# First rows in two transfers, reordered lists and more fillers in an attention and SwiGLU kernel

## The chip, the cores and the metric

The program runs on one core of a Trainium2 chip. The metric is the device time of one launch in microseconds (us). The kernel before took 363.26 us, the median of three runs (363.25 to 364.06 us).

A core has a matrix engine (TensorE, PE in the profile, with its weight loads as PEld), VectorE (DVE), ScalarE (ACT), GpSimd (POOL) and SyncE (SP, which only issues transfers here). Each engine has its own list of instructions and works through it in order; semaphores hold it back where it needs another engine's result or a transfer. TensorE writes into PSUM, from which VectorE and ScalarE copy.

## The reference

Eight batches of eight heads, 576 tokens each, 64 wide, with 16 beacon keys and values ahead of the 576 causal ones; then a SwiGLU block over the 4608 tokens with 512 model and 1536 inner columns. All is float32 in memory.

```python
k_all = np.concatenate([beacon_k, k], axis=2)
v_all = np.concatenate([beacon_v, v], axis=2)
scores = (1 / sqrt(64)) * q @ k_all.T          # 576 x 592 per batch and head
scores = where(causal, -1e9, scores)           # beacons are seen by every row
a = exp(scores - max); a /= a.sum(-1) + 1e-9
x = (a @ v_all) -> [4608, 512]                 # tokens by (head, width)
out = (silu(x @ w_gate) * (x @ w_val)) @ w_out
```

## The kernel before, in words

**Attention.** The work on a batch is cut into four pairs of heads. For each pair the queries and keys come as rows (tile `qk`), TensorE turns them (`turn`, plan letter T, into `t_ps`), and copies bring them into `qT` and `kT` (`turned_copy`: K and Q on VectorE, k and q on ScalarE). Scores are made in units A to D, four to a pair (letters S and s; s adds the causal mask by further matmuls with `ramp` and `against`). ScalarE takes the exponential of a unit (E) into `p`; where a unit wasn't masked by matmuls, a mask multiplies it on VectorE (D) or GpSimd (M). The product with the values (P and p, tile `pv_ps`; Z for the first 240 rows of batch 0, `pvf_ps`) is normalized on VectorE (R, N) into `x`, and turned into `xT` (X, J, V).

**The SwiGLU block.** One gate and value product (G, then H, both halves into `gv_ps`) makes 128 inner columns for up to 512 tokens. ScalarE takes tanh (a), VectorE multiplies twice (1, 2) into `hT`. The projection (F) collects the 12 blocks of inner columns into two banks of `o_ps`, which `evacuate` copies out (O on VectorE, o on ScalarE) and stores. The last pair of token blocks is projected in two parts of 320 and 192 columns, each in its own bank, so that the first part can be copied while the second is computed.

**What sets the order.** There is no scheduler: `plan` is a string of letters, and each letter emits its piece in that order on whatever engines it uses. `order_of_loads` names the loads that the letters L and l issue one after the other on GpSimd's queue (K0.4: keys of batch 0, heads 4 to 7; v0.2: a block of 128 value rows of batch 0; g2, u2: the third part of the gate and val weights). Eight semaphores serve these loads in turn, so the ninth load waits on GpSimd until the first has landed. The letter h asks for one filler, a matmul of the identity that nobody reads; `keep_warm` emits those asked for ahead of the next score unit or value product.

**PSUM.** Four slots of two banks each go round. `take` gives a tile the slot that has been free for longest, `give` returns it. Dependencies are followed by tile; `apart` declares that two instructions of different engines on one tile don't depend on each other, since they touch different banks.

**The opening.** The first 256 rows of heads 0 and 1 come through SyncE's and ScalarE's queues into `first` (L672), those of heads 2 to 7 by GpSimd (L681). The beacons of batch 0 are cast by VectorE (b), turned (W) and copied (e on ScalarE, A on VectorE). From batch 1 on, two heads are first paired side by side (`pair_up`, g on VectorE, f on GpSimd, into `side`), so that one transpose serves both.

Of the kernel before, what the change touches and what calls it, by code (L numbers as in the profile page):

```python
# [84 lines left out]
def kernel(  # L85
# [733 lines left out]
    pSyEGXRHELDSyLDGaELGH1H2aaXD1Lf2Py1pGGLH2GRaXHlylH12aaGGH112a2HG1G2Haa1HaTq2lgGl1H2k1GaS21l2HSEa
    lsElGS12ETHgKQGEaS12lEHlTDa1GSqH2glDkESfaGslE1H2ElSEMDlTGMSQaKEHSMM12aGEs1HEa2T1qPpMllkDPfllSpRE  # L820
    2sRfsPDpSEEFEFFSFRDFFlSElSPEMpTFFlFERkFSfFFlqDSSFFFlEDFDEFSFTEFDFFFSQVlEkEFFDDFFOSEOllFFTtFqKFDl
    MSFESFFFFElSSMDlFElPplPlpERsFDFRFFFEFStlFFEGSGHtFDHDEaGMF1FFaH12POlOpaPp2RlG1GlRHtal2G1HHGVa21ll
    l2ltGHal1G2lGHHa1aatlt21tGH1H2lattF2aGFH112FF2FFGSaEFlHt1GFFaHa2Gltl1t2GtlH12latH12Fa12FFGGtDHSl
    tlaE1FHFFaG2lSFHtl12allF12GFElMFllFHaSG1FEFHaGFFolMHl2l1G2aSOF1H2FaE1FtFG2sHFEaFslF1FDFlSE2FDFED
    FSESlPpFFFRlDFFFlStFESSDFFEFFsEDFOPEpMPEOpSFFlFRMStRFEFEFSsFEMEFFDFFPplFSFFFFFlFRDSSEFEtFtSFDFFF
    FFEEFlVFFsoOElFFSFtFFDFtSMPEDEtSFElpSDRFFMFFtlMPtESSFEEpRFttFFGFDDSEGHFGa12HHlla1aG21FHl2aGlFHl1
    a2GSHD1ool2aDtPlEGM1ltp2HRlla1GtlSlGH2alEGHG1l2FaM1HHF2a1GFa2HS1FF2FSFFaEFSFEF12lFSPEFpDMFEFSlSR
    FFlEFFtSFttEFFDFSFVFFESEtFFFMsMDEFFFDFEsOFSFFolPttDEFDFSpFFEMFsESFRFFFEFFtFPMEGGOtHoSEtaplHRPtla
    11Gpt2HD2tGMRaGSt1HH2tGEa1al2G1HSa2GEH1a2GttHGa12SHH1a2MEG1GaM2DSHHES12FaEFFFFF1FDla2FFPSF1FE2Fp
    RFFSFFSEFSFESFFFFVEFSFFFFDDFEFFEFFDSoFPFFMlFpFEStlFERFFFFFSSDoEPMFFEFFFDDOMGpoRSElPHGa1S2pHEaR1G  # L830
    2sHlGGEDaHaD12GG1Ha2H12aG1Ha2HaGG12S1EHlHGa2a1D2MSH1FEl2GSMFa1H2EMPaFDF1FSF2EDFFFpSFEFFsRFFFSFFF
    SEFPEEFFSFpERFFSFFFMDVFMSFFDEEPFFDSoFFFFpFFFFEFDOFSPRFDFSpEGFFFEGRGDDFHaO1oHH2aa12P1GpRHGGH2VaGH
    a1a12HG2Ga1H122HGa1Ga2G1HHH2aa1a21G21GH2aG12HaHGFFFF1a2FFGF1H2aHaGF1H2FaF1GF2F1GHHFFFaa2FF12G1GH
    aFFFFH12F2FFFFFFaG1FHFFoFaFoFF212GGFHaFF1FHFF2FFaFGFFFFOHoG12GHHFaa12GFaFFF1FFF21FHF2GGFFaHFaFF1
    FFF12FHa2FG1GFHF2HFaF1FoaFFoFFFFFG2FF1FFHFaF1FGFF2HGFFFaFF12FH2FFaFFFFF1FFFFF2oFFFFFFFFFFFFOFFFF
    FFFOFoFFFFFFFFFFFOoFFFFFFOo
# [43 lines left out]
```

## Time and profile before

| | |
|---|---|
| median of three runs | 363.26 us (363.25 to 364.06) |
| profiled execution | 364.0 us, of it the span 362.0 us |
| TensorE busy | 353.9 us, 98% of the span |
| VectorE, ScalarE, GpSimd busy | 223.6, 189.0, 123.8 us |
| gate and val matmuls, 1824 | 406.2 us of modelled time, two running at once |
| projection matmuls, 912 | 116.0 us |
| mean granted clock | 0.995 of full speed |

Busy time of TensorE is the time in which at least one matmul ran; their ends are modelled, and two on different halves of the array overlap. The waits are read from the timeline (the number in brackets behind a row is the idle time ahead of it and what ended it) and from the table by stage, where the length of a stretch less its busy time is the idle time.

### The profile page before, as it was taken

How to read it: one execution, taken by the hardware profiler on the slowest of the kernel's cores; microseconds unless marked ns; L12 is line 12 of the kernel's file. 1: busy time of each engine (PE TensorE's matmuls, PEld its weight loads, DVE VectorE, ACT ScalarE, POOL GpSimd, SP SyncE). 2: the span in 40 equal slices, each digit the busy share in tenths (PEclk: the TensorE clock that was granted, in tenths of full speed). 3: DMA queues.
4: the chain of work that ended last, by engine and by line, in shares of the span. 5: the costliest groups of instructions: out<-in, count | busy, mean ns of one | idle time of the engine just before them, and what ended most of it. 6: DMA issues, size and time to landing. Idle time of an engine off the chain costs nothing.

```text
span 362.0 us, 11854 instructions
## 1 busy us (share of the span) xinstructions
PE 353.9 (98%) x5150; PEld 200.7 (55%) x5150; DVE 223.6 (62%) x437; ACT 189.0 (52%) x286; POOL 123.8 (34%) x185
## 2 busy tenths in 40 slices
PE   7899999999999999999999999999999999999996
PEld 4677566654444566544565556545655554455554
DVE  5577987667766753497518763777467764464341
ACT  4966989822425677543864466546633332331311
POOL 8935489936337544375423013112000000000000
PEclk9899999999999999999999999999999999999999
DMA  8999999999999999999999829602422000110113
GB/s 120 166 204 203 186 194 139 173 176 155 140 153 113 133 137 119 161 115 170 139 120 170 111 28 138 95 0 20 107 78 67 2 2 0 61 58 3 61 60 116
DMA packets 146132, 39.74 MB, mean 110 GB/s; under 512 B 131488, under 2 KB 141728, under 8 KB 146080
## 3 DMA queue, kind: packets, MB, share of 16 engines
q0 software_dynamic: 97424, 19.00, 73.4%
q1 hardware_dynamic: 48368, 19.76, 26.3%
q8 instruction: 40, 0.66, 0.8%
q10 hardware_dynamic: 288, 0.23, 0.2%
q14 instruction: 12, 0.10, 0.1%
HBM read 38.27 MB, written 9.44 MB: 132 GB/s over the span
## 4 chain that ended last, share of the span: by engine, by line
PE 84%; DMA 8%; POOL 4%; issue 3%; ACT 1%; POOLq 0%
PE gv_ps L173 46%; PE o_ps L173 26%; PE s_ps L173 5%; DMA wv<-in_moe_w_val_dram 4%; PE pv_ps L173 4%; PE pv_ps L505 3%; DMA wg<-in_moe_w_gate_dram 2%; DMA qk<-in_q_dram 2%; POOL qk L215 1%; POOL vb L225 1%; ACT p L414 0%; POOL wv L254 0%; POOL p L427 0%; POOL wo L258 0%; PE t_ps L171 0%
## 5 line engine op out<-in xcount | busy, mean ns | idle before, releaser
L173 PE MATMUL gv_ps<-xT,wv 64*128 64x512 bf16 (+2 forms) x912 | 203.2, 365 | 0.6 <-DMA wv<-in_moe_w_val_dram 0.6
L173 PE MATMUL gv_ps<-xT,wg 64*128 64x512 bf16 (+2 forms) x912 | 203.0, 365 | 0.1
L591 ACT ACTIVATE th<-gv_ps 128x512 f32<-128x512 f32 (+2 forms) x114 | 65.4, 575 | 118.0 <-PE gv_ps L173 117.6
L414 ACT ACTIVATE p<-s_ps 128x832 bf16<-128x832 f32 (+2 forms) x127 | 104.6, 869 | 34.4 <-PE s_ps L173 28.7
L173 PE MATMUL o_ps<-wo,hT 64*128 64x512 bf16 (+2 forms) x912 | 116.0, 365 | 0.4 <-ACT p L414 0.4
L596 DVE SCALAR_TENSOR_TENSOR u<-th,gv_ps 128x512 f32<-128x512 f32 (+2 forms) x114 | 74.7, 656 | 66.4 <-ACT th L591 65.7
L173 PEld LDWEIGHTS <-wg 64*128 64x128 bf16 x912 | 82.4, 94 | 45.7 <-PE gv_ps L173 2.4
L173 PEld LDWEIGHTS <-wv 64*128 64x128 bf16 x912 | 81.7, 94 | 40.7 <-DMA wv<-in_moe_w_val_dram 0.7
L603 DVE SCALAR_TENSOR_TENSOR hT<-gv_ps,u 128x512 bf16<-128x512 f32 (+2 forms) x114 | 74.7, 661 | 3.0
L173 PEld LDWEIGHTS <-hT 64*128 64x128 bf16 x912 | 43.4, 94 | 32.8 <-DVE hT L603 0.7
L225 POOL DMA_DIRECT2D vb<-in_v_dram x40 | 33.9, 851 | 63.0 <-PE s_ps L173 25.3
L173 PE MATMUL s_ps<-qT,kT 64*128 64x336 bf16 (+3 forms) x512 | 43.5, 254 | 1.4 <-ACT kT L262 0.8
L173 PEld LDWEIGHTS <-kT 64*128 64x128 bf16 x512 | 23.8, 94 | 22.6 <-issue 1.4
L423 DVE TENSOR_TENSOR p<-p,ramp 128x256 bf16<-128x256 bf16 (+2 forms) x84 | 23.9, 315 | 10.0 <-ACT p L414 9.8
L225 POOL DMA_DIRECT2D qk<-in_q_dram x25 | 21.2, 851 | 25.5 <-DMA qT<-qk 5.8
L534 DVE TENSOR_TENSOR x<-pv_ps,rec 128x640 bf16<-128x640 f32 (+1 forms) x32 | 25.3, 791 | 1.2
L533 DVE RECIPROCAL rec<-pv_ps 128x10 f32<-128x10 f32 (+1 forms) x32 | 6.8, 213 | 28.8 <-PE pv_ps L173 22.8
L225 POOL DMA_DIRECT2D qk<-in_k_dram x25 | 21.2, 851 | 5.7 <-PE gv_ps L173 4.4
L427 POOL TENSOR_SCALAR_AFFINE_SELECT p<-p 128x256 bf16<-128x256 bf16 (+2 forms) x46 | 17.5, 402 | 13.6 <-ACT p L414 13.3
L263 DVE COPY o_sb<-o_ps 128x512 f32<-128x512 f32 (+2 forms) x18 | 11.6, 657 | 16.5 <-PE o_ps L173 16.5
L173 PEld LDWEIGHTS <-p 64*128 64x128 bf16 x960 | 18.7, 94 | 4.5 <-PE pv_ps L173 0.2
L173 PE MATMUL pv_ps<-vb,p 64*128 64x65 bf16 x960 | 19.9, 189 | 0.0
(63 smaller groups left out, 142.8 us busy)
## 6 DMA issues: line engine op xcount, KB each, us to landing
out_dram<-o_sb SPq DMA_DIRECT2D x34, 256.0 KB, 3.6
vb<-in_v_dram POOLq DMA_DIRECT2D x24, 128.0 KB, 5.8
qk<-in_q_dram POOLq DMA_DIRECT2D x21, 128.0 KB, 5.2
qk<-in_k_dram POOLq DMA_DIRECT2D x16, 128.0 KB, 5.8
wo<-in_moe_w_out_dram POOLq DMA_DIRECT2D x2, 768.0 KB, 9.8
wg<-in_moe_w_gate_dram POOLq DMA_DIRECT2D x3, 384.0 KB, 14.9
wv<-in_moe_w_val_dram POOLq DMA_DIRECT2D x3, 384.0 KB, 13.7
qk<-in_k_dram POOLq DMA_DIRECT2D x2, 576.0 KB, 11.9
```

What stands on the lines that cost most here:

```text
L173: ins = nc.tensor.matmul(o, lhsT=l, rhs=r, start=start, stop=stop)
L225: return nc.gpsimd.dma_start(dst[p0 : p0 + n, c, :, 0:D], src[b, :, r : r + n, :].rearrange("h j d -> j h d"))
L263: return eng.tensor_copy(o, i)
L414: nc.scalar.activation(p_of(b, m, u == "A")[:, :, c0 : c0 + w], ps[:, :, 0:w], ACT.Exp, scale=0.125)
L423: nc.vector.tensor_tensor(out=ap, in0=ap, in1=upper[:, None, d : d + w].to_broadcast([P, 2, w]), op=ALU.mult)
L427: nc.gpsimd.affine_select(out=ap, in_=ap, compare_op=ALU.is_ge, fill=0.0, base=d, pattern=[[0, 2], [1, w]], channel_multiplier=-1,)
L505: ins = nc.tensor.matmul(o_ps[:, side, 68 * c : 68 * c + D + 1], lhsT=pt[n % NPT][:, side, col : col + P], rhs=vb[b % 2][:, t, 2 * m + sid ...
L533: nc.vector.reciprocal(rec[:, :, c0:NKT], o[:, :, :, D : D + 1])
L534: nc.vector.tensor_tensor(out=xs[b][:, c0:NKT, P * m : P * m + P].rearrange("p c (h d) -> p h c d", d=D), in0=o[:, :, :, 0:D], in1=rec[:, ...
L591: nc.scalar.activation(th[:, 0:w], gvs[n][:, 0, 0:w], ACT.Tanh, scale=0.5)
L596: nc.vector.scalar_tensor_tensor(out=u[:, 0:w], in0=ths[n][:, 0:w], scalar=1.0, in1=gvs[n][:, 0, 0:w], op0=ALU.add, op1=ALU.mult)
L603: nc.vector.scalar_tensor_tensor(out=hTs[j][:, f, c0:c1], in0=gvs.pop(n)[:, 1, 0 : c1 - c0], scalar=0.5, in1=ths.pop(n)[:, 0 : c1 - c0], o ...
```

## The change

The first rows of heads 2 to 7 come in two transfers (keys, queries) for four. The plan is ordered anew from its start to about a quarter; behind its first 448 letters (458 now), about 77 us into the span, it is letter for letter the old one. The order of the first 56 loads changes too. In that part the plan has twenty fillers for ten, three key copies more on VectorE and one query copy fewer (three key copies fewer on ScalarE, one query copy more), two copies into `xT` on VectorE that were ScalarE's, five masks on GpSimd that were VectorE's, one paired copy more on GpSimd, and the beacon copy on VectorE. All other letters stand in the same number. The calls of `apart` in `project` and `evacuate` are gone, and `halves` returns nothing.

```diff
@@ halves
         newest[0] = ins.ins.name
-        return ins
@@ project
-                ins = halves(
+                halves(
                     key, at, row, ps[:, at, cols],
 ...
-                if at:
-                    apart(ins, copied.get((key, 0), []))
@@ evacuate
-        ins = copy(eng, o_sb[:, cols], ps[:, at, cols])
-        apart(ins, copied.get((key, 1 - at), []))
-        copied[key, at] = [ins]
+        copy(eng, o_sb[:, cols], ps[:, at, cols])
@@ opening
-    for h0, h1 in ((2, 4), (4, H)):
+    for h0, h1 in ((2, H),):
         runs(0, k, h0, h1, 0, FRONT)
         runs(0, q, h0, h1, 0, FRONT)
@@ order_of_loads
-    K0.0 Q0.0 v0.2 Q0.4 K0.4 v0.1 v0.0 v0.3 v0.4 v0.5 g1 u0 g0 u1 g2 u2 K1 Q1 b1 u3 g3 g4 u4 Q2 v1.5 K2 v1.3
+    v0.0 Q0.0 K0.0 Q0.4 v0.1 K0.4 v0.2 v0.4 v0.3 v0.5 u1 u0 g1 g0 g2 u2 Q1 K1 b1 g3 u3 u4 v1.5 g4 v1.2 v1.0 K2
 ...
@@ plan
-    0LhbTqLLhhWKehTQsLTLEKLsqLkELhhSLTcQsKELKEsLssQEshsEhDELshEEELLhLTQZkNZsNSPpJEEILsJPLLERIpSXLDRP
+    0bWTAqkhhhhsTLLLELcqKThhsqKhhhSTELELqKsDsEKLEhshsQEEsZThsNhhhsEQhhZLLLEKLEsLPpNESREJhhsIELSJPDLp
 ...
```

**TensorE, from the ninth score unit of batch 0 to the first value product.** `s_ps` are scores, `t_ps` the turn of the last key and query rows, `pvf_ps` the value product of the first rows; DMASW0 to DMASW7 are the semaphores of GpSimd's loads. Before:

```order
L187 MATMUL s_ps<-ident 128x256 [waits Activation_49]
L173 LDWEIGHTS kT_107
L173 MATMUL s_ps<-qT_105,kT_107 128x336
...
L171 LDWEIGHTS qk_101 [waits DMASW0_49]
L171 MATMUL t_ps<-ident,qk_101 64x64 [waits Activation_49]
...
L446 LDWEIGHTS p_109 [waits DMASW2_49]
L446 MATMUL pvf_ps<-vb_103,p_109 128x65 [waits DMASW1_49]
...
L446 MATMUL pvf_ps<-vb_103,p_109 128x65 [waits DMASW6_49]
```

And now:

```order
L173 MATMUL s_ps<-against,ramp 128x16
L445 LDWEIGHTS p_109 [waits DMASW6_49]
L445 MATMUL pvf_ps<-vb_103,p_109 128x65 [waits DMASW2_49]
...
L445 MATMUL pvf_ps<-vb_103,p_109 128x65 [waits DMASW0_49]
...
L171 LDWEIGHTS qk_101 [waits DMASW7_49]
L171 MATMUL t_ps<-ident,qk_101 64x64 [waits Activation_49]
...
L186 MATMUL s_ps<-ident 128x256 [waits Activation_49]
L173 LDWEIGHTS kT_107
L173 MATMUL s_ps<-qT_105,kT_107 128x336
```

The value product stands ahead of the turn and of the ninth and tenth score units, no longer behind them. Its last wait, DMASW0, is for the second value block (v0.2).

**GpSimd, the first loads.** Before, in the order in which they are issued behind the first rows of heads 4 to 7:

```order
L215 DMA qk_101<-in_k_dram 64x4x320
L215 DMA qk_101<-in_q_dram 64x4x320
L225 DMA vb_103<-in_v_dram 128x8x64
...
L225 DMA vb_103<-in_v_dram 112x8x64 [waits DMASW1_49]
L225 DMA vb_103<-in_beacon_v_dram 16x8x64 [waits DMASW2_49]
```

And now, from the first transfer on:

```order
L214 DMA qk_101<-in_k_dram 64x6x256
L214 DMA qk_101<-in_q_dram 64x6x256
...
L224 DMA vb_103<-in_beacon_v_dram 16x8x64
L214 DMA qk_101<-in_q_dram 64x4x320
...
L224 DMA vb_103<-in_v_dram 112x8x64
L214 DMA qk_101<-in_k_dram 64x4x320
L224 DMA vb_103<-in_v_dram 128x8x64 [waits DMASW0_49]
```

The 128 value rows (v0.2) move from the third place of the list to the seventh, where the values of the beacons stood; the same six loads are then ahead of the seventh.

**TensorE, the last matmuls.** The last of 320 columns and the first of 192. Before:

```order
L173 MATMUL o_ps<-wo,hT 128x320
L173 LDWEIGHTS hT [waits PE_49]
L173 MATMUL o_ps<-wo,hT 128x192
L173 LDWEIGHTS hT
L173 MATMUL o_ps<-wo,hT 128x192
```

And now:

```order
L173 MATMUL o_ps<-wo,hT 128x320
L173 LDWEIGHTS hT [waits PE_49]
L173 MATMUL o_ps<-wo,hT 128x192 [waits DVE_49]
L173 LDWEIGHTS hT [waits PE_49]
L173 MATMUL o_ps<-wo,hT 128x192 [waits Activation_49]
```

The order is the same; the first matmul into the second part of either tile now waits for VectorE and for ScalarE, which are the copies of the 320 columns.

## Rows read from the trace of the kernel before

**Rows 1.** The page: busy tenths of TensorE in 40 slices of the span.

```profile
PE   7899999999999999999999999999999999999996
```

**Rows 2.** By stage: window, length, busy us (count) by engine, PEclk, DMA, GB/s.

```profile
8.00:10.00 2.00, 1.16 (x48) 0.62 (x46) 0.14 (x1) 2.00 (x4) 2.00 (x4) 1.00 1.54 141
11.50:15.00 3.50, 3.50 (x82) 2.27 (x78) 0.80 (x4) 3.50 (x5) 2.90 (x5) 0.51 2.20 154
25.00:27.00 2.00, 1.44 (x31) 1.18 (x29) 1.69 (x5) 0.19 (x1) 0.00 (x0) 1.00 1.22 209
50.00:60.00 10.00, 9.23 (x202) 6.62 (x203) 7.91 (x16) 8.30 (x14) 9.99 (x17) 1.00 1.71 170
60.00:150.00 90.00, 89.94 (x1250) 49.19 (x1247) 56.26 (x109) 50.31 (x72) 49.16 (x69) 1.00 1.71 148
```

**Rows 3.** The waits of TensorE: total, times, longest us.

```profile
PE pv_ps L505 <- POOL p L427: 0.4, 1, 0.4
```

**Rows 4.** Timeline of GpSimd: start, us, engine, line, operation, idle before.

```profile
1.33 0.71 POOL L215 DMA_DIRECT2D qk<-in_k_dram  x1 [0.81 <-POOLq L864]
...
3.24 0.64 POOL L215 DMA_DIRECT2D qk<-in_q_dram  x1
...
8.53 0.57 POOL L225 DMA_DIRECT2D vb<-in_beacon_v_dram  x1
...
15.89 0.76 POOL L254 DMA_DIRECT2D wv<-in_moe_w_val_dram  x1
...
31.63 1.14 POOL L263 COPY side<-qk 128x1152 bf16<-128x1152 bf16 x1 [7.78 <-DMA qk<-in_q_dram]
```

**Rows 5.** Transfers issued at 3.24, 8.53 and 15.89 us: KB, us to landing.

```profile
qk<-in_q_dram POOLq DMA_DIRECT2D x1, 128.0 KB, 3.9
...
vb<-in_beacon_v_dram POOLq DMA_DIRECT2D x1, 16.0 KB, 5.9
...
wv<-in_moe_w_val_dram POOLq DMA_DIRECT2D x1, 384.0 KB, 10.2
```

**Rows 6.** Timeline of ScalarE, fifth to tenth exponential and the copy behind them.

```profile
11.47 4.81 ACT L414 ACTIVATE p<-s_ps 128x832 bf16<-128x832 f32 x6
16.11 0.77 ACT L262 ACTIVATE kT<-t_ps 128x640 bf16<-128x640 bf16 x1
```

**Rows 7.** Timeline of TensorE: fillers, scores, turn, value product, fourth gate product.

```profile
5.96 0.61 PE L187 MATMUL s_ps<-ident 128*128 128x256 bf16 x4
...
12.84 0.57 PE L173 MATMUL s_ps<-qT,kT 64*128 64x336 bf16 x4
...
14.34 0.75 PE L171 MATMUL t_ps<-ident,qk 64*64 64x64 bf16 x40
...
15.25 0.71 PE L446 MATMUL pvf_ps<-vb,p 128*128 128x65 bf16 x18
...
16.93 0.21 PE L173 MATMUL s_ps<-qT,kT 64*128 64x80 bf16 x2 [0.28 <-ACT kT L262]
...
26.18 0.27 PE L173 MATMUL gv_ps<-xT,wv 64*128 64x240 bf16 x1 [0.56 <-DMA wv<-in_moe_w_val_dram]
```

**Rows 8.** Timeline of VectorE, a copy of the turn and a normalization.

```profile
15.14 0.82 DVE L263 COPY qT<-t_ps 128x640 bf16<-128x640 bf16 x1 [2.84 <-PE t_ps L171]
...
16.11 0.76 DVE L462 TENSOR_TENSOR x<-pvf_ps,rec 128x256 bf16<-128x256 f32 x2
```

**Rows 9.** Timeline of VectorE and ScalarE, one pair of output copies.

```profile
319.53 0.69 DVE L263 COPY o_sb<-o_ps 128x512 f32<-128x512 f32 x1 [2.27 <-PE o_ps L173]
319.53 0.60 ACT L262 ACTIVATE o_sb<-o_ps 128x512 f32<-128x512 f32 x1 [2.21 <-PE o_ps L173]
```

**Rows 10.** Timeline of the end: matmuls of 192 columns, copies of 320.

```profile
357.35 0.49 PE L173 MATMUL o_ps<-wo,hT 64*128 64x192 bf16 x7
...
357.56 0.49 DVE L263 COPY o_sb<-o_ps 128x320 f32<-128x320 f32 x1 [1.92 <-PE o_ps L173]
357.60 0.44 ACT L262 ACTIVATE o_sb<-o_ps 128x320 f32<-128x320 f32 x1 [2.05 <-PE o_ps L173]
```

More of the change, by code (lines that the diff above doesn't have):

```diff
@@ L734 @@
     order_of_loads = """
-    K0.0 Q0.0 v0.2 Q0.4 K0.4 v0.1 v0.0 v0.3 v0.4 v0.5 g1 u0 g0 u1 g2 u2 K1 Q1 b1 u3 g3 g4 u4 Q2 v1.5 K2 v1.3
-    v1.2 v1.0 v1.1 v1.4 b2 o0 o1 v2.2 k3.0 v2.1 q3.2 v2.5 k3.5 v2.4 v2.3 v2.0 q3.4 q3.0 q4.2 k4.0 v3.3 k3.1 q4.0
-    k3.4 k3.2 q3.1 v3.0 k4.2 q3.3 k4.3 v3.5 q4.4 k3.3 v3.4 v3.2 k4.5 k4.1 q4.3 q4.1 v4.1 v4.5 v4.3 v4.0 k4.4
+    v0.0 Q0.0 K0.0 Q0.4 v0.1 K0.4 v0.2 v0.4 v0.3 v0.5 u1 u0 g1 g0 g2 u2 Q1 K1 b1 g3 u3 u4 v1.5 g4 v1.2 v1.0 K2
+    Q2 v1.1 b2 v1.4 v1.3 o0 o1 v2.4 v2.5 v2.3 q3.0 v2.2 k4.0 v2.1 v2.0 k3.2 q3.4 k3.0 k3.1 v3.3 v3.0 q3.3 q3.2
+    k3.5 q3.1 q4.0 q4.2 k4.2 k3.4 k4.3 v3.5 q4.4 k3.3 v3.4 v3.2 k4.5 k4.1 q4.3 q4.1 v4.1 v4.5 v4.3 v4.0 k4.4
     v3.1 v4.2 q6.1 k5.0 q5.1 q5.4 k5.3 k5.5 k6.0 k5.2 k5.1 q5.0 k6.2 q5.3 v4.4 k6.1 q6.0 q6.2 k6.5 q5.2 v5.2
@@ L817 @@
     plan = """
-    0LhbTqLLhhWKehTQsLTLEKLsqLkELhhSLTcQsKELKEsLssQEshsEhDELshEEELLhLTQZkNZsNSPpJEEILsJPLLERIpSXLDRP
[L819 to L836, printed above, removed]
+    0bWTAqkhhhhsTLLLELcqKThhsqKhhhSTELELqKsDsEKLEhshsQEEsZThsNhhhsEQhhZLLLEKLEsLPpNESREJhhsIELSJPDLp
+    SILERPSpGEGLHRXLHLEaMMMYaGLX1HLLa21P2yX12pGGRHLlXyGHYGHLHa12a1l2Ga1f2a1GHaHaGf21122Ha1GTl2qHTlGK
@@ new lines @@
+    ak1LqHf2hSa1SGEEsD2ElHTlGflQMlaSk1lEHS2TDQGESlKaE1H2SGasEE1HGaS2SMHEEf1aGSMMHM2s1DlEPa2S1pEl2EPs
+    RlDEpsPTERqpKMlSEFFFSRfgEMFFSlFlTPplElkQSRVlEFMSEFllFDFFSEgFTFFFDqSSFFFDKEFSFFFFEEFSFOFFSllEOllF
+    EDtFTSMQDlDlFFEKllFlSEFFPpFDSPEptFRRstMSMlDEEDFFFlFFFDFSGGFFEHaHD1FaG2FFH1POlOpaPp2RlG1GlRHtal2G
+    1HHGVa21lll2ltGHal1G2lGHHa1aatlt21tGH1H2lattF2aGFH112FF2FFGSaEFlHt1GFFaHa2Gltl1t2GtlH12latH12Fa1
+    2FFGGtDHSltlaE1FHFFaG2lSFHtl12allF12GFElMFllFHaSG1FEFHaGFFolMHl2l1G2aSOF1H2FaE1FtFG2sHFEaFslF1FD
@@ new lines @@
+    FlSE2FDFEDFSESlPpFFFRlDFFFlStFESSDFFEFFsEDFOPEpMPEOpSFFlFRMStRFEFEFSsFEMEFFDFFPplFSFFFFFlFRDSSEF
+    EtFtSFDFFFFFEEFlVFFsoOElFFSFtFFDFtSMPEDEtSFElpSDRFFMFFtlMPtESSFEEpRFttFFGFDDSEGHFGa12HHlla1aG21F
+    Hl2aGlFHl1a2GSHD1ool2aDtPlEGM1ltp2HRlla1GtlSlGH2alEGHG1l2FaM1HHF2a1GFa2HS1FF2FSFFaEFSFEF12lFSPEF
+    pDMFEFSlSRFFlEFFtSFttEFFDFSFVFFESEtFFFMsMDEFFFDFEsOFSFFolPttDEFDFSpFFEMFsESFRFFFEFFtFPMEGGOtHoSE
+    taplHRPtla11Gpt2HD2tGMRaGSt1HH2tGEa1al2G1HSa2GEH1a2GttHGa12SHH1a2MEG1GaM2DSHHES12FaEFFFFF1FDla2F
@@ new lines @@
+    FPSF1FE2FpRFFSFFSEFSFESFFFFVEFSFFFFDDFEFFEFFDSoFPFFMlFpFEStlFERFFFFFSSDoEPMFFEFFFDDOMGpoRSElPHGa
+    1S2pHEaR1G2sHlGGEDaHaD12GG1Ha2H12aG1Ha2HaGG12S1EHlHGa2a1D2MSH1FEl2GSMFa1H2EMPaFDF1FSF2EDFFFpSFEF
+    FsRFFFSFFFSEFPEEFFSFpERFFSFFFMDVFMSFFDEEPFFDSoFFFFpFFFFEFDOFSPRFDFSpEGFFFEGRGDDFHaO1oHH2aa12P1Gp
+    RHGGH2VaGHa1a12HG2Ga1H122HGa1Ga2G1HHH2aa1a21G21GH2aG12HaHGFFFF1a2FFGF1H2aHaGF1H2FaF1GF2F1GHHFFFa
+    a2FF12G1GHaFFFFH12F2FFFFFFaG1FHFFoFaFoFF212GGFHaFF1FHFF2FFaFGFFFFOHoG12GHHFaa12GFaFFF1FFF21FHF2G
@@ L837 @@
+    GFFaHFaFF1FFF12FHa2FG1GFHF2HFaF1FoaFFoFFFFFG2FF1FFHFaF1FGFF2HGFFFaFF12FH2FFaFFFFF1FFFFF2oFFFFFFF
+    FFFFFOFFFFFFFOFoFFFFFFFFFFFOoFFFFFFOo
     """
```

## The prediction

> **What bounds the kernel now.** I read the slices first: after the first two, TensorE is at 9 tenths everywhere but in the last [rows 1]. The table by stage says how little stands open: from 60 to 150 us TensorE is idle for 0.06 us of 90, while it loses 0.84 us from 8 to 10 us, 0.56 us from 25 to 27 us and 0.77 us from 50 to 60 us [rows 2]. The program is bound by TensorE's own work, which the change leaves alone but for ten fillers; what it can win is the idle time ahead of about 77 us, where the two lists become equal, and what it can lose is any new wait. Third the list of waits: one for a mask on GpSimd cost 0.4 us [rows 3]. Last the timelines of the places that the order shows to move.
>
> 0.3% of 363.26 us, about what a measurement can tell here, is 1.1 us: below that I call it no change.
>
> **The opening transfers.** Four transfers for the first rows of heads 2 to 7 become two. GpSimd issues the four from 1.33 to 3.88 us, so its next work comes about 1.2 us sooner (two issues of 0.6 us) [rows 4]. The last of them lands at 3.24 + 3.9 = 7.1 us [rows 4, 5]. The two carry the same bytes in the same pieces, and from 8 us on the DMA share is above 1 in every row [rows 2], so I take 7.1 us for the second of the two as well: gain 0, at best 0.6 us (one issue), at worst a loss of 1.2 us, because heads 2 and 3, which had their own early transfers, now wait for those of all six heads, two issues more. The new list turns them behind the first score unit, so the loss is covered.
>
> The Trainium skill (DMA: Bandwidth & Descriptors, Anatomy of one DMA) gives each transfer of this kind a fixed cost of about 2.0 us, and by that rule two transfers fewer would free up to 4 us; here four of them were issued and landed within 5.8 us, bytes included, so the fixed parts overlap and the rule's saving is not to be had in series. By it the sum would be up to 4 us lower, by the row it is unchanged.
>
> **ScalarE relieved.** Key and query copies go to VectorE; the largest that leaves ScalarE here is 0.77 us at 16.11 us [rows 6]. Until the fourth exponential the new list gives ScalarE other copies instead (the first key copy and two query copies for one key copy and the beacons'), so I let the row of six exponentials start where it does, at 11.47 us: 0, bounds -0.4 and +0.4. From there ScalarE is the pace maker: six in 4.81 us, 0.80 us each, the fourth done at 14.7 us.
>
> **The front's value product moved ahead of the turn.** This is the first place that I count. Before, TensorE does two more score units (12.84 us on), the turn of the last key and query rows (14.34) and only then the first value product of batch 0 (15.25) [rows 7]; its value rows are then all there, the seventh load of the list landing at 8.53 + 5.9 = 14.4 us [rows 4, 5]. Afterwards the product stands in front of the turn and of both score units, and the load that it needs last, the second value block, is now the seventh of the list, behind the same bytes: 14.4 us again. TensorE reaches it about when it ended the eighth score unit before, 12.6 us, and waits some 1.8 us in order, with everything behind it. Then: rest of the product 0.25, turn 0.6 (0.75 in the row, partly at the lower clock), filler and score 0.5, so the ninth exponential starts near 15.75 instead of 14.7 us; the ninth and tenth scores, fillers and the second product reach to 17.0; VectorE has two copies of 0.82 us behind the first normalization (1.0 us, of it 0.76 us for the multiplies) [rows 8] and, starting at 14.65 us, is ready at 17.2 us, against 16.93 us before [rows 7]. So TensorE comes out 0.4 us late there, and with the two fillers left (0.15 us each by four in 0.61 us [rows 7]) 0.4 + 0.3 = 0.7 us late at the fourth gate product. All other fillers stand in waits for copies; if these covers were gone, ten cost 1.5 us.
>
> **What hides it.** The fourth gate product waited 0.56 us until 26.18 us for val weights that landed at 15.89 + 10.2 = 26.1 us [rows 4, 5, 7]. That load keeps its place (16th, the same 15 ahead), and the DMA queues are full, so it lands at 26.1 us again (bounds 25.5 and 26.5). Of the 0.7 us late, 0.6 is thus paid out of that wait: net +0.1 us, and equally, whatever the front wins is lost there.
>
> **The clock.** TensorE idled 0.84 us between 8 and 10 us, and from 11.5 to 15 us its granted clock is 0.51, the lower level; while it waited 0.56 us at 26 us and 0.77 us in all in the fifties it stayed at 1.00 [rows 2]. The fillers close the first hole, but the new wait of 1.8 us is longer than any of these. If the clock falls behind it for 3.5 us as in the row, work for 1.75 us at the full clock takes twice the time, and now TensorE, not ScalarE, is the one waited for: +1.75 us at most, 0 if it stays up. I take 0.8 us, near the middle, as the fall looks a little likelier than not and part of it lies beside copies.
>
> The Trainium skill (TensorE: Matmul & The Clock Gate, HAM oscillation) tells of the clock falling where a wait for DMA stands between short bursts of matmuls; the row at 11.5 us agrees, and by that rule the new wait brings the full 1.75 us, so the sum would be 0.95 us higher.
>
> **Batch 1's turns.** The first paired copy is ready when keys and queries have landed: GpSimd starts it at 31.63 us for 1.14 us [rows 4]. The second was on VectorE beside it and is now behind it on GpSimd, done at 33.9 us, and both turns stand closer together. TensorE comes there 0.9 us later than before by the terms above; +0.1 us, bounds 0 and 0.8. Five masks go from VectorE to GpSimd, three of them before GpSimd's long idle time (7.78 us ahead of 31.63 [rows 4]): hidden, 0. The other two fall where GpSimd is busy for 9.99 of 10 us [rows 2], but two paired copies have left that stretch for an earlier one: 0, bounds -0.9 (both waits of the fifties gone) and +0.8.
>
> **The evacuations.** The diff also drops the declarations that the two banks of an output tile are independent, and the order shows what that makes. Where ScalarE and VectorE empty the two banks together, as at 319.53 us, one now waits 0.6 to 0.7 us for the other. There both had been idle for over 2 us [rows 9], TensorE waited for neither: 0, bounds 0 and 1.2 (two such places in mid-kernel more). The end is different: the last 24 matmuls of 192 columns, which began at 357.35 us beside the copies of the tile's other part, now wait for them, until 358.05 (357.56 + 0.49) on VectorE and 358.04 on ScalarE [rows 10]. Nothing is behind to hide it: +0.7 us, bounds 0.5 and 0.9.
>
> **Sum.** 0.1 + 0.8 + 0.1 + 0.7 = +1.7 us on the profiled execution's 364.0 us (362.0 of span, 2.0 around it), 365.7 us. That execution stood 0.74 us above the median of the runs, 363.26 us, so there it is **365.0 us**.
>
> **Rivals.**
> - The clock stays up. The fillers speak for it, and the two later holes that didn't lower it. Then the sum is 0.9 us, 364.2 us: no measurable change.
> - The front wins. ScalarE has less to do and the fillers keep the clock up; if the val weights landed before 25.5 us, the 0.56 us there and the 0.77 us of the fifties and the odd 0.2 go: 363.26 - 1.5 + 0.7 = 362.5 us, and 361.8 us if the last matmuls don't wait either. Against it the full queues and the unchanged place of the load. It decides from the landing of that load on, not from ScalarE's end of exponentials, which may well come earlier without use.
> - GpSimd becomes late in the fifties. It has no room there; two masks and later loads of batch 1 and 2 behind paired copies make TensorE wait twice more as it did for 0.4 us [rows 3], with the terms above 366.0 to 366.5 us.
> - The transfers don't do what they say: with the second landing after 8 us the score units of heads 2 and 3 start 0.9 us late; ScalarE's row starts late with them, but ends before the val weights all the same. It changes only how the wait at 26 us is filled.
>
> **Chances.** Forecast 0.45, clock up 0.27, the front wins 0.14, GpSimd late 0.14. Slower by over 0.3%: most of the first, a third of the second, all of the fourth, 0.64. Faster by over 0.3% only if the front wins and the end waits less than I think: 0.07. Within: 0.29. The range for 8 in 10 goes from 363.4 (most of what the front may win, but not with a free end) to 366.8 us (full cost of the clock and one later wait).
>
> **What would show it.** A gap of TensorE ahead of the second part of the front's first value product, ended by a v load near 14.4 us; a granted clock near 0.5 in some stretch between 14 and 20 us; the fourth gate product starting at 26.2 to 27.5 us; the last 192-column matmuls starting at 358.05 us on the shifted scale, 0.7 us behind the last of 320 columns, released by the output copies; no idle between 80 us and there. The forecast is wrong if the gate product starts before 25.5 us, if the gap at the end is missing, or if idle time of over 1.5 us shows between 30 and 77 us.

## The result, and the profile after

The changed kernel takes 365.25 us (median of 7 runs, 364.71 to 366.19) beside 363.49 us for the kernel before (7 runs, 362.83 to 364.06): a ratio of 1.0055, with a 95% interval of 1.0039 to 1.0071. A second measurement gave 1.0041 (1.0029 to 1.0053). So it is slower by 1.5 to 1.8 us, where 1.7 us was forecast. The profiled execution took 366.19 us (span 364.2 us) and was the longest of its seven, which matters below.

The page's slices, TensorE's busy tenths and its granted clock, answer to [rows 1]. Only the second and the last slice of TensorE differ from the row before.

```profile
PE   7999999999999999999999999999999999999995
PEclk9999999999999999999999999999999999999998
```

The table by stage (window, length, busy us and count by engine, PEclk, DMA, GB/s) answers to [rows 2].

```profile
8.00:10.00 2.00, 2.00 (x65) 1.34 (x62) 1.00 (x5) 1.07 (x3) 2.00 (x3) 1.00 1.67 170
11.50:15.00 3.50, 3.07 (x100) 2.37 (x98) 1.68 (x5) 3.50 (x7) 3.50 (x6) 1.00 2.05 172
25.00:27.00 2.00, 2.00 (x44) 1.49 (x41) 1.67 (x6) 0.95 (x3) 2.00 (x3) 1.00 1.22 205
50.00:60.00 10.00, 9.54 (x229) 7.38 (x228) 8.44 (x17) 8.30 (x12) 6.99 (x10) 1.00 1.38 151
60.00:150.00 90.00, 90.00 (x1252) 48.79 (x1248) 58.32 (x115) 50.14 (x70) 50.42 (x72) 1.00 1.76 148
```

Every hole that the prediction counted is smaller. From 8 to 10 us TensorE is busy for 2.00 us where it had 1.16 (at half the rate, as the next rows show), the clock from 11.5 to 15 us is 1.00 where it had 0.51 (TensorE idles there for 0.43 us), the 0.56 us from 25 to 27 us are gone, and the fifties lose 0.46 us for 0.77. And yet the end is later. The loss is outside these windows, in the first 8 us and in the last 5.

TensorE's timeline of the opening (start, us, line, operation, times, idle before and what ended it) answers to [rows 7]:

```profile
6.73 0.39 PE L171 MATMUL t_ps<-ident,beacons 64*128 64x64 bf16 x4 [1.44 <-DVE beacons L275]
7.05 0.43 PE L171 MATMUL t_ps<-ident,qk 64*64 64x64 bf16 x16
7.41 1.04 PE L186 MATMUL s_ps<-ident 128*128 128x256 bf16 x4
...
8.38 0.49 PE L173 MATMUL s_ps<-qT,kT 64*128 64x240 bf16 x4
...
14.53 0.54 PE L445 MATMUL pvf_ps<-vb,p 128*128 128x65 bf16 x12
```

The first turn of the program is now the beacons', and TensorE stands idle for 1.44 us ahead of it. The four fillers behind it take 1.04 us, where four took 0.61 us [rows 7]: they run at about half the rate, though the column PEclk reads 1.00 there. That is no fall of the clock behind the wait: the rate had not risen yet. In every profile the program opens with warming matmuls of 512 columns, and those from 1.67 to 4.2 us start 0.42 or 0.43 us apart, that is 1.2 columns per ns, the lower level. Their last four, of 128 columns, show whether the rate rose (ns of one: lowest, median, highest; start of the first and the last; changed kernel, then kernel before):

```profile
L688 PE MATMUL idle_ps<-p x5: 314/314/634, 4.2 to 5.0; 128*128 128x128 bf16 x4, 128*128 128x512 bf16 x1
L693 PE MATMUL idle_ps<-p x5: 219/219/627, 4.2 to 4.9; 128*128 128x128 bf16 x4, 128*128 128x512 bf16 x1
```

In the changed kernel they are still at the lower level, and so are the matmuls behind the wait. The first record of the clock in its trace stands at 10.49 us, where the matmuls reach the full rate (4.72 us in the kernel before); ahead of the first record the column reads 1.00 whatever the rate.

The front's first value product (14.53) doesn't wait at all. VectorE's timeline and the transfers show what held the beacons (transfers: operation, KB, us from issue to landing):

```profile
5.77 0.90 DVE L275 CAST beacons<-first_beacons 16x512 bf16<-16x512 f32 x1 [1.28 <-DMA first_beacons<-in_beacon_k_dram]
```

```profile
first_beacons<-in_beacon_k_dram SPq DMA_DIRECT2D x1, 32.0 KB, 4.1
```

```profile
first_beacons<-in_beacon_k_dram SPq DMA_DIRECT2D x1, 32.0 KB, 3.1
```

The second fence is of the changed kernel, the third of the kernel before. Both issue this 32 KB transfer at 1.60 us; it landed at 4.7 us before and at 5.7 us after. The cast of the same shape then took 0.90 us. The other loads came sooner: value block v0.2, issued at 6.99 us, and the val weights, issued at 14.02 us, took

```profile
vb<-in_v_dram POOLq DMA_DIRECT2D x1, 128.0 KB, 5.5
```

```profile
wv<-in_moe_w_val_dram POOLq DMA_DIRECT2D x1, 384.0 KB, 10.1
```

so they landed at 12.5 and 24.1 us, where [rows 5] give 14.4 and 26.1 us for the loads in these places of the list.

The end, which answers to [rows 10]:

```profile
359.02 0.49 DVE L262 COPY o_sb<-o_ps 128x320 f32<-128x320 f32 x1 [1.92 <-PE o_ps L173]
359.06 0.44 ACT L261 ACTIVATE o_sb<-o_ps 128x320 f32<-128x320 f32 x1 [1.32 <-PE o_ps L173]
359.57 1.17 PE L173 MATMUL o_ps<-wo,hT 64*128 64x192 bf16 x24 [0.58 <-DVE o_sb L262]
360.75 0.36 DVE L262 COPY o_sb<-o_ps 128x192 f32<-128x192 f32 x1 [1.24 <-PE o_ps L173]
```

The copies of 320 columns are 1.46 us later than before (359.02 for 357.56), the matmuls of 192 columns 2.22 us (359.57 for 357.35), and they name VectorE's output copy as what they waited for. So of 2.2 us of span in this pair of profiles, 1.46 had arisen before (1.26 of it by VectorE's first output copy, at 65.17 for 63.92 us) and 0.76 arose here.

### The profile page after: what moved, and what is told of

Read it like the earlier page. It is cut to its first block, busy times and chain, and to the rows that moved or that the text cites. A ratio compares the mean times of both kernels' runs of the same rounds, so it can differ in the third digit from the quotient of the medians.

```text
span 364.2 us, 11880 instructions
## 1 busy us (share of the span) xinstructions
PE 355.9 (98%) x5160; PEld 201.0 (55%) x5160; DVE 224.7 (62%) x437; ACT 186.1 (51%) x279; POOL 126.2 (35%) x190
## 4 chain that ended last, share of the span: by engine, by line
PE 93%; ACT 2%; POOL 1%; DMA 1%; issue 1%; DVE 1%; SPq 0%; POOLq 0%; ACTq 0%
PE gv_ps L173 51%; PE o_ps L173 26%; PE s_ps L173 7%; PE pv_ps L173 4%; PE pv_ps L504 4%; DMA first_beacons<-in_beacon_k_dram 1%; PE t_ps L171 1%; ACT p L413 1%; PE s_ps L186 1%; POOL side L262 1%; POOL qk L214 0%; PE xt_ps L547 0%; DVE beacons L275 0%; SPq L668 0%; DVE hT L602 0%
## 5 line engine op out<-in xcount | busy, mean ns | idle before, releaser
L173 PE MATMUL s_ps<-qT,kT 64*128 64x336 bf16 (+3 forms) x512 | 42.7, 251 | 0.5 <-ACT qT L261 0.4
L426 POOL TENSOR_SCALAR_AFFINE_SELECT p<-p 128x256 bf16<-128x256 bf16 (+2 forms) x52 | 19.9, 405 | 20.3 <-ACT p L413 20.1
L422 DVE TENSOR_TENSOR p<-p,ramp 128x256 bf16<-128x256 bf16 (+2 forms) x78 | 20.5, 294 | 7.3 <-ACT p L413 7.2
L262 DVE COPY o_sb<-o_ps 128x512 f32<-128x512 f32 (+2 forms) x18 | 11.6, 658 | 20.8 <-PE o_ps L173 17.8
## 6 DMA issues: line engine op xcount, KB each, us to landing
qk<-in_q_dram POOLq DMA_DIRECT2D x2, 576.0 KB, 10.7
```

The lines of the kernel that those rows point to most:

```text
L173: ins = nc.tensor.matmul(o, lhsT=l, rhs=r, start=start, stop=stop)
L262: return eng.tensor_copy(o, i)
L422: nc.vector.tensor_tensor(out=ap, in0=ap, in1=upper[:, None, d : d + w].to_broadcast([P, 2, w]), op=ALU.mult)
L426: nc.gpsimd.affine_select(out=ap, in_=ap, compare_op=ALU.is_ge, fill=0.0, base=d, pattern=[[0, 2], [1, w]], channel_multiplier=-1,)
```

## The experiments

Each was timed beside the kernel before; intervals are of the ratio to it. One reading helps throughout: in every profile VectorE's first output copy, at 63 to 65 us, stands 299.5 to 300.1 us ahead of the execution's time where the declarations of `apart` are in, and 300.6 to 301.1 us where they are not. So an execution is told by two numbers, where that copy stands (the front) and which of the two groups it is in (the end). The front differs much between executions of one order: that copy stands at 63.02, 63.92 and 64.71 us in the three profiles with the old opening, and at 63.40, 64.37 and 65.17 us in the three with the whole new one. What the front costs is therefore taken from many runs, and no pair of profiles shows it.

### The declarations put back

```diff
+                ins = halves(
+                if at:
+                    apart(ins, copied.get((key, 0), []))
...
+        ins = copy(eng, o_sb[:, cols], ps[:, at, cols])
+        apart(ins, copied.get((key, 1 - at), []))
+        copied[key, at] = [ins]
```

> The changed kernel with the declarations that keep the buffers of the two evacuating engines apart put back; nothing else. Theory A (the end costs 0.74 us because the last 24 matmuls of 192 columns wait for the copies of 320 columns): the first of these matmuls begins about 0.7 us earlier against the 320-column copies, the rest is unmoved, time 364.5 us, that is 0.7 us below the changed kernel and about 1.0 to 1.4 us above the kernel before (ratio 1.003 to 1.004). Rival (the end is late for another reason, the waits of the output copies on one another being only where it is booked): time within 0.2 us of the changed kernel, ratio 1.005 to 1.006.

Measured: 364.36 us (12 runs), ratio 1.0014 (1.0001 to 1.0026), 0.9 us below the changed kernel's first measurement and 0.7 below its second. The size of the end fits theory A; the ratio is under its 1.003 to 1.004, as the front costs less than it had. The end, which in this kernel runs through without a gap (the last copies of 192 columns wait 0.50 us for matmuls that were never held):

```profile
357.16 0.49 DVE L263 COPY o_sb<-o_ps 128x320 f32<-128x320 f32 x1 [1.92 <-PE o_ps L173]
...
358.15 0.36 DVE L263 COPY o_sb<-o_ps 128x192 f32<-128x192 f32 x1 [0.50 <-PE o_ps L173]
```

What is left, 0.7 us over the kernel before by the medians and 0.5 by the ratio, is the front alone.

### The declarations taken from the kernel before

The same edit the other way, in the kernel before.

> The kernel before without the declarations that keep the buffers of the two evacuating engines apart; nothing else. Theory A: the opening is unmoved, the last 24 matmuls begin 0.7 us later, time 0.7 us above the kernel before (ratio 1.002). Rival 1: the pairs of copies through the kernel, now one after the other, cost too, and the time rises by 1.5 us or more (ratio 1.004 or more). Rival 2: the end does not wait, ratio 1.000.

Measured: 364.41 us (12 runs) for 363.66, ratio 1.0017 (1.0007 to 1.0028): +0.75 us, as theory A had it. The gap is there:

```profile
358.46 0.49 DVE L262 COPY o_sb<-o_ps 128x320 f32<-128x320 f32 x1 [1.92 <-PE o_ps L173]
358.49 0.44 ACT L261 ACTIVATE o_sb<-o_ps 128x320 f32<-128x320 f32 x1 [1.32 <-PE o_ps L173]
359.00 1.17 PE L173 MATMUL o_ps<-wo,hT 64*128 64x192 bf16 x24 [0.58 <-DVE o_sb L262]
```

The pairs of copies in mid-kernel cost nothing: from VectorE's first output copy to the one near 225 us it is 160.70 us in the kernel before and 160.71 us here. Rival 1 falls.

### Keys and queries turned ahead of the beacons

```diff
-    0bWTAqkhhhhsTLLLELcqKThh
+    0bTWqkAhhhhsTLLLELcqKThh
```

> The changed kernel with the first turn of q and k tiles, and its two copies, ahead of the beacons' turn, in which the changed list has it behind. Theory B (TensorE's first real work waits for the beacons, which land at 5.7 us where they landed at 4.7, and the order of the list makes everything wait with it): the first q and k turn begins near 5.2 us, the first scores near 6.5 us, the output copies through the kernel stand 1.0 to 1.4 us earlier than in the changed kernel, time 364.0 to 364.3 us (ratio 1.0015 to 1.002). Rival 1 (the list behind the opening costs the front, not its first steps): copies shift by under 0.3 us, ratio 1.005. Rival 2 (the turn goes first but the beacons, still late, hold the next step): half of it, 0.5 to 0.7 us.

With the declarations put back as well:

> The changed kernel with both: the q and k turn ahead of the beacons' turn, and the declarations that keep the evacuating engines' buffers apart. Theories A and B together: 0.74 us off the end and 1.0 to 1.4 us off the front, time 363.1 to 363.5 us, no different from the kernel before or up to 0.1% faster (ratio 0.999 to 1.000). Rival (part of the front's loss lies in the order behind the opening): 364.0 us or more, ratio 1.0015 or more.

Measured: 365.07 us (6 runs), 1.0042 (1.0027 to 1.0057), and 363.94 us (12 runs), 1.0005 (0.9991 to 1.0019). The order of the two turns is thus worth 0.2 us (beside the changed kernel; none beside its second measurement) and 0.4 us (beside the one with the declarations), no more than a measurement tells, and less than theory B's 1.0 to 1.4 us. The second kernel can't be told from the one before. TensorE's timeline of the first of them, and then of the second:

```profile
4.88 0.32 PE L171 MATMUL t_ps<-ident,qk 64*64 64x64 bf16 x16
6.14 0.29 PE L171 MATMUL t_ps<-ident,beacons 64*128 64x64 bf16 x4 [0.95 <-DVE beacons L275]
...
12.64 0.24 PE L445 MATMUL pvf_ps<-vb,p 128*128 128x65 bf16 x2
13.60 0.46 PE L445 MATMUL pvf_ps<-vb,p 128*128 128x65 bf16 x10 [0.72 <-DMA vb<-in_v_dram]
```

```profile
5.90 0.39 PE L171 MATMUL t_ps<-ident,beacons 64*128 64x64 bf16 x4 [0.25 <-DVE beacons L276]
...
12.61 0.24 PE L446 MATMUL pvf_ps<-vb,p 128*128 128x65 bf16 x2
13.16 0.46 PE L446 MATMUL pvf_ps<-vb,p 128*128 128x65 bf16 x10 [0.32 <-DMA vb<-in_v_dram]
```

Here is the step that the prediction had in the wrong size. With the opening out of the way TensorE reaches the value product at 12.6 us, the forecast's number, and does wait for a v load, but for 0.72 and 0.32 us and not 1.8: the rows land at 13.1 to 13.6 us, not 14.4. In the changed kernel's second profile (below) TensorE came at 12.94 us, did not wait and began the next turn at 13.45 us; here it began it at 13.99 and 13.56 us. So what the earlier opening wins is lost there again, which fits the small return of turning the two steps round.

### Four transfers again

```diff
-    for h0, h1 in ((2, H),):
+    for h0, h1 in ((2, 4), (4, H)):
```

> The changed kernel with the first rows of heads 2 to 7 in four transfers, as in the kernel before; list and copies as changed. Theory B1 (the beacons land late because the two larger transfers, issued ahead of or beside them, take the queues): beacons land near 4.7 us, their cast takes 0.4 us, TensorE's first turn begins near 5.2 us, output copies 1.0 us or more earlier, but the value weights land near 26.1 us again and take up to 0.5 us of that back; time 364.2 to 364.8 us. Rival (the beacons are late for their place in the list of issues, not for the size of the transfers beside them): beacons at 5.7 us, time 365.2 us or, with the value weights late as well, up to 365.8 us.

With the two edits above:

> The changed kernel with the q and k turn first, the declarations back, and four transfers for the first rows: what is left of the change is the list behind the opening, the key and query copies on VectorE and the fillers. Theory B1: beacons at 4.7 us, nothing waits in the opening, the value weights at 26.1 us hold the fourth gate product by up to 0.6 us: ratio 0.999 to 1.001. Rival (the two transfers carry a gain of the list, the earlier stream): 0.5 us or more above the same kernel with two transfers. Rival 2 (the list behind the opening loses by itself, by the front value product that stands earlier and waits until 14.4 us, and by a clock that falls behind it): ratio 1.002 or more, with a wait of over 1 us ahead of that product in the trace.

And the reverse, two transfers in the kernel before:

> The kernel before with the first rows of heads 2 to 7 in two transfers; its list, copies and declarations unmoved. Theory B1 (the two larger transfers delay the beacons by 1.0 us): beacons land near 5.7 us, but in this list the first q and k turn stands ahead of the beacons' turn, so that only the second step waits, by 0.7 to 1.0 us; the value weights land near 24.1 us and the wait of 0.56 us for them is gone. Sum +0.1 to +0.5 us (ratio 1.000 to 1.0015). Rival 1 (two transfers are harmless to the beacons): the wait of 0.56 us goes, ratio 0.9985. Rival 2 (the whole front loss comes from the transfers): ratio 1.004.

Measured: 365.59 us (5 runs), 1.0050 (1.0038 to 1.0063); 365.68 us (12 runs), 1.0055 (1.0029 to 1.0082), which is 1.7 us above the same kernel with two transfers; and 364.02 us (12 runs), 0.9995 (0.9977 to 1.0013). Theory B1's gain is not there; with the new list four transfers are no better, and in the second kernel clearly worse. Four transfers land the beacons at 4.6 us in the first (1.60 + 3.0) and 5.5 us in the second, but the next keys come late. TensorE in the two kernels with four:

```profile
10.24 0.51 PE L171 MATMUL t_ps<-ident,qk 64*64 64x64 bf16 x40 [0.60 <-DMA qk<-in_k_dram]
```

```profile
10.83 0.51 PE L171 MATMUL t_ps<-ident,qk 64*64 64x64 bf16 x40 [1.30 <-DMA qk<-in_k_dram]
```

The turn of forty tiles waits 0.60 and 1.30 us for key rows; with two transfers it did not wait (9.54 to 9.93 us in five profiles). In the second kernel the clock then falls too (window, length, busy, count, PEclk, DMA, GB/s):

```profile
11.50:15.00 3.50, 3.22 (x51) 0.58 2.30 160
```

A part of the 1.7 us is this fall. Over the second kernel's twelve runs the mean granted clock of the span was at least 0.998 in five (median 364.52 us), 0.994 or 0.995 in three (365.47 to 366.03 us) and 0.990 or 0.991 in four (367.66 to 367.85 us); with two transfers it was at least 0.998 in eleven of twelve (median 363.94 us). At an equal clock 0.6 us are left.

In both kernels with four the value rows and the val weights land late too: v0.2 at 14.10 and 14.87 us (12.5 to 13.7 us in the eight profiles with two), the val weights at 24.8 and 25.5 us (23.3 to 24.2 us). So with the two edits the new list needs the two transfers; without them (365.59 beside 365.25 and 365.10 us) the difference isn't clear of noise, and in the old list there is none.

### Beacons first on their queue

```diff
+    nc.sync.dma_start(
+        first_beacons[:].rearrange("j (h d) -> j h d", d=D), beacon_k[0].rearrange("h j d -> j h d")
+    )
...
-    nc.sync.dma_start(
-        first_beacons[:].rearrange("j (h d) -> j h d", d=D), beacon_k[0].rearrange("h j d -> j h d")
-    )
```

> The changed kernel with the beacons' transfer issued ahead of the first keys on the same queue. Theory B: the beacons land at 4.0 to 4.7 us, their turn begins near 5.2 us, the keys land some 0.3 us later than now, the first scores begin near 7.0 us instead of 8.4 us, time 364.0 us (1.2 us below the changed kernel, ratio 1.0015). Rival (the first keys are as late by it as the beacons were, and the front waits for these): under 0.4 us, ratio 1.0045 or more.

Measured: 366.05 us (6 runs), 1.0054 (1.0033 to 1.0074): no gain. The beacons landed 1.8 us after their issue, but the first keys now took 4.5 us, and VectorE casts the keys before the beacons. VectorE's two casts, and TensorE behind them:

```profile
5.88 0.67 DVE L262 CAST qk<-first 128x256 bf16<-128x256 f32 x1 [2.12 <-DMA first<-in_k_dram]
6.47 0.40 DVE L275 CAST beacons<-first_beacons 16x512 bf16<-16x512 f32 x1
```

```profile
6.93 0.29 PE L171 MATMUL t_ps<-ident,beacons 64*128 64x64 bf16 x4 [1.90 <-DVE beacons L275]
```

```profile
9.00:11.50 2.50, 2.50 (x65) 0.51 1.85 160
```

In this profile too the second transfer on that queue is the late one, as the rival had it; the wait is 1.90 us, and the granted clock behind it is 0.51. Here the rate had risen by the end of the warming matmuls, so this is a fall. The Trainium skill (TensorE: Matmul & The Clock Gate, HAM oscillation) has the clock fall where TensorE waits for DMA between short bursts of matmuls; the waits of its example are about 3 to 5 us. This row and the one behind the wait of 1.30 us above agree with it, at shorter waits; waits of 0.82 to 0.95 us in three other profiles were not followed by a fall, and the one at 11.5 us in the kernel before [rows 2] came behind waits of 0.50 us at most:

```profile
8.84 0.33 PE L173 MATMUL s_ps<-qT,kT 64*128 64x240 bf16 x4 [0.50 <-ACT kT L262]
```

So the length of one wait alone doesn't decide. The slow stretch behind 1.44 us in the changed kernel is no case of it.

### The value product moved back

```diff
-    ...QEEsZThsNhhhsEQhhZ...
+    ...QEEsThsZNhhhsEQhhZ...
```

> The changed kernel with the q and k turn ahead of the beacons' turn, the declarations back, and the first half of the front's value product moved back behind the next turn and the next score unit (about 1.1 us later on TensorE). In the run with the first two edits alone that product began at 12.61 us and stood still for 0.32 us until v rows landed. Theory C (the value product stands too early in the changed list, as the prediction had it, and what it loses is passed on): its wait goes, the copies through the kernel stand 0.2 to 0.5 us earlier, time 363.3 to 363.7 us, ratio 0.998 to 0.9995. Rival (another operand is late next, or the clock in the opening decides more than the wait): no gain, ratio 1.000 to 1.001.

Measured: 364.51 us (12 runs), 1.0040 (1.0017 to 1.0063): slower by 0.6 us in the median than with the product in the changed list's place, so theory C falls, though the intervals of the two kernels touch (1.0017 to 1.0019). TensorE:

```profile
13.43 0.35 PE L171 MATMUL t_ps<-ident,qk 64*64 64x64 bf16 x20 [0.47 <-issue]
...
14.29 0.54 PE L446 MATMUL pvf_ps<-vb,p 128*128 128x65 bf16 x12
15.93 0.50 PE L187 MATMUL s_ps<-ident 128*128 128x256 bf16 x3 [1.09 <-DVE x L462]
```

The wait for v rows is gone, and one of 1.09 us for VectorE's normalization takes its place, which starts at 14.87 us for 13.66 us. ScalarE, waiting for the scores behind it, stands 1.39 us. But 0.47 us of the delay is a gap in the turn ahead of the product, and there is another later; the profile names no engine or load that either waited for (the last section says what such gaps are likely to be):

```profile
56.13 0.40 PE L505 MATMUL pv_ps<-vb,p 128*128 128x65 bf16 x8 [0.88 <-issue]
```

Such gaps come to 1.36 us here and to 0.43 us in the profile with the product in the changed list's place, and the first output copies are 1.28 us apart (65.11 for 63.84 us). So the later place brings no gain; that the early one is a gain isn't shown.

### More warming matmuls

```diff
-    warm(8, TOK)
+    warm(12, TOK)
```

> The changed kernel with 12 idle matmuls of 512 columns at the start for 8; it computes the same. In the changed kernel TensorE stood idle from 5.28 to 6.73 us until the beacons were there, and the matmuls behind it ran at half the rate until about 9.8 us; in the run with the declarations back, with the same opening, the idle time was 0.91 us and they ran at the full rate. Theory D (the idle time behind the warming matmuls is what the slow stretch follows from): the added matmuls end at 6.0 to 6.4 us, the matmuls behind the beacons' turn run at the full rate in the profile, and the time is 364.4 to 364.8 us, 0.4 to 0.9 us below the changed kernel. Rival (the slow stretch comes or doesn't come whatever stands there, or the added matmuls hold the beacons' turn): 365.0 to 365.7 us.

Measured: 365.63 us (6 runs), 1.0060 (1.0040 to 1.0080). TensorE:

```profile
6.73 0.29 PE L171 MATMUL t_ps<-ident,beacons 64*128 64x64 bf16 x4
...
7.20 0.61 PE L186 MATMUL s_ps<-ident 128*128 128x256 bf16 x4
```

The fillers take 0.61 us: the rate rose at 6.22 us, while the added matmuls ran, and the matmuls behind the beacons' turn have the full rate, as theory D wanted. The full rate stood behind the eight matmuls as well in two other profiles of this opening, so one profile doesn't show that the added ones brought it. The beacons' turn is no earlier, and there is no gain. The beacons landed late in this profile (their cast ended at 6.67 us), so it doesn't tell whether the added matmuls held the turn too.

### Both kernels once more

> The changed kernel once more, for a second profile and a ratio on this chip. Theory E (its opening differs from one execution to the next, by the landing of the beacons and by whether a slow stretch of TensorE follows): beacons' turn between 5.9 and 6.8 us, ratio 1.003 to 1.006, single times spread over 1.5 us. Rival (the opening seen in its first profile is its steady one): beacons' turn at 6.7 us and fillers of 1.04 us behind it again.

> The kernel before once more, for a second profile. Theory E: the slow stretch that its first profile shows from 11.5 to 15 us is in another place or missing, and the output copies stand up to 1 us elsewhere, with the beacons at 4.7 us as in every run with four transfers but one. Rival: the same stretch at half the clock again, copies within 0.2 us of the first profile.

Measured: 365.10 us (5 runs), 1.0041 (1.0029 to 1.0053), and 363.12 us (one run). The changed kernel's second profile, TensorE:

```profile
5.89 0.29 PE L171 MATMUL t_ps<-ident,beacons 64*128 64x64 bf16 x4 [0.82 <-DVE beacons L275]
...
6.36 0.61 PE L186 MATMUL s_ps<-ident 128*128 128x256 bf16 x4
...
12.94 0.54 PE L445 MATMUL pvf_ps<-vb,p 128*128 128x65 bf16 x12
```

and the kernel before's second:

```profile
5.97 0.39 PE L171 MATMUL t_ps<-ident,beacons 64*128 64x64 bf16 x4 [0.33 <-DVE beacons L276]
...
6.66 1.04 PE L187 MATMUL s_ps<-ident 128*128 128x256 bf16 x4
...
7.62 0.49 PE L173 MATMUL s_ps<-qT,kT 64*128 64x240 bf16 x4
```

The opening differs from one execution to the next in both. The changed kernel's beacon turn starts at 5.89 us here, without a slow stretch behind it (0.61 us for four fillers), and the time is 365.28 us; the first profile showed a bad opening: 0.9 us in time, 0.8 us at the first output copy. The spread that theory E wanted is seen over both measurements (364.71 to 366.19), not in these five runs (364.85 to 365.28). The kernel before ran at the lower rate from the start this time: the clock's first record stands at 10.09 us. Its first scores were 1.1 us later than in the first profile (7.62 for 6.50), and it was still 0.9 us faster. It had no wait for val weights, which landed at 24.83 us, and lost 0.19 us in the fifties for 0.77. Its beacons landed at 5.5 us, so a late landing isn't a matter of the two transfers alone.

So the rate of the opening is a chance of the execution in both kernels. In seven of the fourteen profiles it had not risen by the end of the warming matmuls. In four of these it rose at 5.3 to 6.5 us, with waits of 0.25 us at most ahead of it; in three (the first of the changed kernel, the second of the kernel before, and the kernel before with two transfers) at 10.1 to 10.7 us, with 1.44, 0.33 and 0.40 us as the longest wait ahead of it.

## Why the prediction was right, and where it was wrong

The value was right (365.0 for 365.25 and 365.10 us), the side too. The end was right in mechanism and size. The front's terms, 1.0 us, came near the measured 0.5 to 0.7 us, but neither the clock's 0.8 nor the value product's 0.1 came about as put down: that the sum fits is luck. Of the signs that the prediction named, the gap at the end and the fourth gate product at 26.2 to 27.5 us are there (27.29 and 26.71 us in the two profiles, without a wait); the gap ahead of the value product and the low clock between 14 and 20 us are not.

- **The end, +0.7.** The trace gives 0.76, taking the declarations from the kernel before +0.75 us, putting them back in the changed one -0.7 to -0.9. The step held as written.
- **The evacuations in mid-kernel, 0.** Held: 160.70 and 160.71 us.
- **The opening transfers, 0.** The second of the two landed at 2.11 + 4.8 = 6.9 us, as assumed, and in the old list they make no difference. Three things were missed. GpSimd's next work comes 1.1 us sooner (its next load is issued at 3.19 us for 4.29), and the prediction, with the queues full, gave that no effect on the landings behind it; it had one, as the next two points say. The prediction followed the merged rows and not the beacons, whose turn the new list puts first: TensorE waits for them for 0.82 to 1.44 us at the start, a wait that the sum did not have. And in the new list four transfers make a turn wait for 0.60 and 1.30 us.
- **The value product, net +0.1.** The step that failed is "14.4 us again": v0.2 lands at 12.5 to 13.7 us in the kernels with two transfers. With the new list and four it lands at 14.1 and 14.9 us, so the landing hangs on the transfers ahead and not on the place in the list alone. TensorE, held by the beacons, came at 12.94 and 14.53 us and did not wait; with the turns exchanged it came at 12.6 us and waited for 0.3 to 0.7 us. Moving the product back brought no gain.
- **What hides it, 0.6 paid.** "That load lands at 26.1 us again" failed too: it landed at 24.1 and 24.2 us, and there was no wait to pay out of. But 26.1 us was one execution's value: in the two other profiles of the old list with four transfers the same load landed at 24.24 and 24.83 us, without a wait. So a part of this hole was a chance of the profile that the prediction was read from.
- **The clock, +0.8.** A stretch at the lower rate did stand behind a new wait in one of the two profiles, behind the beacons and not between 14 and 20 us; it was the rate of the start that had not risen yet, and no fall. In the other it did not come. It does in the kernel before too, so it is no cost of the change by itself. A fall as the prediction meant it, behind a wait that a load caused, came in two of the experiments (1.30 and 1.90 us). The Trainium skill (TensorE: Matmul & The Clock Gate, HAM oscillation), which it put beside this, has waits of about 3 to 5 us in its example, so the full 1.75 us did not follow from it for a wait of 1.8 us; and of the waits ahead of its row at 11.5 us the longest, 0.50 us, was for a copy of ScalarE and only one of 0.34 us for a load.
- **The fillers, 0.3.** Ten more of them take 0.11 us each (0.61 us for four, 0.39 us for two), 1.1 us in all. They close waits, and what of them isn't in a wait lengthens the front. I didn't separate this.
- **Batch 1's turns and the fifties, +0.1 and 0.** One wait of 0.3 us for a paired copy on GpSimd in the changed profiles; the fifties lose 0.46 and 0.24 us in its two profiles, 0.77 and 0.19 us in those of the kernel before: no cost. The rival of a late GpSimd did not come; its 366.0 to 366.5 us is more than its own terms give (365.0 and two waits of 0.4 us, 365.8 us).

The front measured by itself, with the declarations in, is +0.7 us by the medians and +0.5 by the ratio (interval 0.0 to 0.9), where the terms gave 1.0. With the two turns exchanged it is +0.1 us (-0.3 to +0.7). The order of beacons and keys holds 0.0 to 0.4 us of it by the medians, which the intervals don't settle; how the rest divides among the fillers, the v load, the chance of the opening and the gaps without a named wait (last section) is open. No version tried beats both kernels: the changed list with both edits is at 1.0005, the kernel before with two transfers at 0.9995, neither of them told from 1.

## What to carry to other kernels

When a list is ordered anew, look at what stands first and follow its own transfer to its landing, even one of 32 KB whose turn had waited 0.33 us at most before: the first wait of an in-order engine is passed on to all behind it, until a later wait takes it up. A landing time read from one trace belongs to that execution and its stream: the val weights landed at 24.2, 24.8 and 26.1 us in three executions of one order. Give it bounds of that width, and work the sum out at both. And profile each kernel twice before explaining a microsecond at the start: two executions of one kernel differed there by 0.8 to 0.9 us, more than the front's share of the change.
